# A PSUM tile of its own for each pair of output blocks, in a two-layer half-product stage on one NeuronCore

## The chip, the cores and the metric

The kernel runs on one core of one Trainium2 chip. The metric is device time in microseconds (us); the time given for a kernel is the median of its runs.

## What is computed

An attention with soft-capped scores feeds two feed-forward networks. Everything is float32 in and out.

```
q, k, v: (4 batches, 12 heads, 448, 64)
scores = cap * tanh(q k^T / 8 / cap);  attn = softmax(scores);  x = attn v -> (1792, 768)
h = x @ w_in (768 x 2048);  g = 0 | h | (h+1)^2/4 by range;  y = g @ w_out (2048 x 768)
m = max(y @ w1, y @ w2, y @ w3) (each 768 x 768);  out = m @ w_out2 (768 x 768)
```

## The kernel before

All activations are kept transposed: features in the 128 partitions, the 448 tokens of a batch in the free dimension. A matrix product in full precision is made of three TensorE products of rounded parts: high by high, high by low, low by high (three matmuls of a 128 x 128 weight block by a 128 x 448 operand). The high part is a copy to the type fp32r, the low part the difference.

The four batches come in three stretches. Batch 0 and then batch 1 run through `ffn`, block by block. Batches 2 and 3 (`last_two`) go through the four layers together, in `strassen`: each layer's product of 2 x 2 blocks is made of seven half products instead of eight, in seven stages. The rows of the two batches are the two halves of the tokens; output block m and output block m + n/2 make one **pair**. In `strassen` the pairs of a layer are taken in groups of three (`threes`): layer 0 has eight pairs (groups of 3, 3 and 2), layer 1 three, layer 2 nine, layer 3 three, which makes eight groups. In each of a group's seven stages every pair gets its own sum over K2 blocks of the operand (3 in layers 0, 2 and 3, 8 in layer 1), so a pair's share of a stage is 9 matmuls, or 24 in layer 1 (there in two runs of 12, with the other pairs between them).

Each pair has two accumulators in PSUM, chosen by `BANK = (0, 1, 0, 0, 1, 0, 1)`: stages 0, 2, 3 and 5 add into accumulator 0, stages 1, 4 and 6 into accumulator 1, "the second partial result". The pool `m` has three slots of one bank; accumulator 0 is an `m` tile for each pair (`ps_m` in the profile). Accumulator 1 comes from the pool `s`, which has two slots of two banks each (`ps_s`): one tile of two banks for two pairs, pair 0 in its first bank and pair 1 in its second, and another for pair 2. The attention stretches use the same pools: `s` for the scores, `a` (one slot of one bank, `ps_a`) for the products with v, `m` for row sums. After each stage each pair's sum is read out of PSUM ("landed", function `lander` and its like in `land_m`): stages 1, 4 and 6 by a VectorE addition or subtraction of two tensors (`plus`, recorded at the helper's line 261), stages 0, 2, 3 and 5 by a copy (line 256 on ScalarE, 258 on VectorE) or a VectorE maximum.

The weights of a stage are streamed (`stream`): a DMA on SyncE's queue brings a piece into a `wf` tile, a copy makes its high part in a `w` tile (line 256 or 258) and a VectorE subtraction its low part (line 261, `w<-wf,w`). There are four `w` slots; a piece feeds 18 or 9 matmuls, in layer 1 it feeds 12. The operands' own parts (`op`) are made once per layer by the same two operations (`divide`).

The order on every engine is planned ahead of time by `Plan`: operations have a cost, a due time (`want`) and dependencies, buffers are taken from pools in the order of their due times, and the planned order is written out as it is. In `strassen` a matmul operation depends on its operand, its weights, the earlier matmuls of its accumulator and the last landing of that accumulator of the same pair (`reads[i][x]`). The waits between engines are put in below the plan, by the framework, from which tiles an instruction reads and writes.

Of the kernel before, what the change touches and what calls it, by code (L numbers as in the profile page):

```python
# [20 lines left out]
class Plan:  # L21
# [29 lines left out]
    def op(self, cost, fn, want, deps=(), uses=(), takes=(), kind=None):  # L51
        o = Plan.Op()
        o.kind = kind
        o.cost, o.fn, o.want = cost, fn, want
        o.deps, o.takes = [d for d in deps if d is not None], list(takes)
        o.uses = list(dict.fromkeys([*uses, *takes]))
        for b in o.uses:
            b.users += 1
        for b in o.takes:
            self.order[b.pool].append((want, len(self.ops), b))  # L60
        o.n, o.out, o.t0, o.t1, o.e = 0, [], None, None, None
        self.ops.append(o)
        return o
# [131 lines left out]
def kernel(  # L195
# [17 lines left out]
    B, H, _, _, S = qk.shape  # L213
    D = 64
    P = 128
# [23 lines left out]
    def buf(p, name, shape, dtype=F32):  # L239
        return plan.buf(p, lambda: pools[p].tile(shape, dtype, tag=p, name=name))  # L240
# [725 lines left out]
    def strassen(layer, pos, swap, blocks, groups, land):  # L966
# [8 lines left out]
        def at(p):  # L975
            return begins(SOLO) + p * PART
# [67 lines left out]
        def stream(stage, pieces, w):  # L1044
            kind = STAGES[stage]
            n = RUN[layer]
            wf, wt = buf("wf", "wf", [P, WU]), buf("w", "w", [P, 2, WU], F32R)
            total = n * len(pieces)
            deps = []
            for m, r in pieces:  # L1050
                if kind[0] == "S":
                    deps.append(summed[layer, m, r][1][int(kind[1]) - 1])
                else:
                    deps.append(stored[corner(layer, m, int(kind[1]) - 1, int(kind[2]) - 1, r)[0]])

            def load(e):
                for x, (m, r) in enumerate(pieces):
                    if kind[0] == "S":
                        src = summed[layer, m, r][0][int(kind[1]) - 1]
                    else:  # L1060
                        u, o = corner(layer, m, int(kind[1]) - 1, int(kind[2]) - 1, r)
                        src = scratch[u][:, o : o + n]
                    nc.sync.dma_start(out=wf.tile[:, x * n : (x + 1) * n], in_=src)

            got = op({"Q": 1.7 * total / 1000}, load, w - 20, deps, takes=[wf])
            hi = op(
                c_copy(total / 1000),
                lambda e: copy(e, wt.tile[:, 0, :total], wf.tile[:, :total]),
                w - 9, [got], [wf], [wt],
            )  # L1070
            lo = op(
                c_tt(total / 1000),
                lambda e: tt(
                    e, wt.tile[:, 1, :total], wf.tile[:, :total], f32(wt.tile[:, 0, :total]),
                    ALU.subtract,
                ),
                w - 8, [got, hi], [wf, wt],
            )
            return wt, [hi, lo]

        for g, group in enumerate(groups):
            A = [buf("m", "ps_m", [P, 512]) for _ in group]
            wide = [buf("s", "ps_s", [P, 2, 512]) for _ in range((len(group) + 1) // 2)]

            def bank(x, i, A=A, wide=wide):
                if x == 0:
                    return A[i], (lambda: A[i].tile[:, :S])
                return wide[i // 2], (lambda: wide[i // 2].tile[:, i % 2, :S])

            taken = {}  # L1090
            last = [[None, None] for _ in group]
            reads = [[[], []] for _ in group]
            state = [land(m, g, i) for i, m in enumerate(group)]
            for stage in range(7):
                x = BANK[stage]
                begun = x == 0 and stage > 0 or stage == 6
                jobs = [(i, r) for r in range(runs) for i in range(len(group))]
                step = max(1, WU // RUN[layer])
                pos_ = starts[g][stage]
                ends = [None] * len(group)  # L1100
                for c in range(0, len(jobs), step):
                    piece = jobs[c : c + step]
                    wt, wops = stream(stage, [(group[i], r) for i, r in piece], at(pos_))
                    for y, (i, r) in enumerate(piece):
                        b_, get = bank(x, i)
                        for q in range(per):
                            k = r * per + q
                            a, aops = operands[stage][k]

                            def fn(e, y=y, q=q, a=a, k=k, get=get, wt=wt, begun=begun):  # L1110
                                o = y * RUN[layer] + q * P
                                wh, wl = (wt.tile[:, z, o : o + P] for z in range(2))
                                h, l_ = a.tile[:, 0], a.tile[:, 1]
                                start, stop = not begun and k == 0, k == K2 - 1
                                for z, (w_, x_) in enumerate(((wh, h), (wh, l_), (wl, h))):
                                    nc.tensor.matmul(  # L1116
                                        get(), w_, x_, start=start and z == 0,
                                        stop=stop and z == 2, skip_group_check=begun,
                                    )

                            deps = [*aops, *wops, *reads[i][x]]
                            if last[i][x] is not None:
                                deps.append(last[i][x])
                            take = [] if id(b_) in taken else [b_]
                            if not take:
                                deps.append(taken[id(b_)])
                            o = op(
                                {"T": PART}, fn, at(pos_), deps, [wt, a, b_], take, "layer",
                            )
                            last[i][x] = o  # L1130
                            taken.setdefault(id(b_), o)
                            pos_ += 1
                        ends[i] = o
                for i in range(len(group)):
                    b_, get = bank(x, i)
                    w = at(starts[g][stage] + (i + 1) * K2) + 0.1
                    r = state[i](stage, get, b_, ends[i], w)
                    reads[i][x] = [r] if r is not None else []
# [47 lines left out]
    def last_two():  # L1186
# [7 lines left out]
        def land_g(m, g, i):  # L1194
# [4 lines left out]
            return lander(G[m], G[m + NF // 2], int(swap), finish)  # L1199

        pos = strassen(0, 0, swap, blocks, threes(N2[0]), land_g)


# [4 lines left out]
        def land_y(m, g, i):  # L1208
# [3 lines left out]
            return lander(Y[m], Y[m + H2], int(swap), finish)  # L1212

        pos = strassen(1, pos, swap, list(zip(G, gdone)), threes(N2[1]), land_y)


# [4 lines left out]
        def land_m(x, g, i):  # L1221
# [45 lines left out]
            return go  # L1267

        pos = strassen(2, pos, swap, list(zip(Y, ydone)), threes(N2[2]), land_m)


# [73 lines left out]
```

## Time and profile before

| | before |
|---|---|
| median of 3 runs | 1025.92 us (1024.76 to 1026.2) |
| the profiled execution: time | 1023.67 us |
| the profiled execution: span from first to last instruction | 1021.5 us |
| TensorE (PE) busy | 984.8 us, 96% |
| VectorE (DVE) busy | 878.4 us, 86% |
| ScalarE (ACT) busy | 603.9 us, 59% |

The profile is of one execution. PE's busy time is made of matmul records that overlap: a matmul's record is longer than the distance to the next one, so a busy share near 100% is no proof that the matmuls stand as close as they can. Times within the trace are counted from the span's start.

### The profile page before, as it was taken

What the parts mean: (1) busy time and instruction counts of PE and PEld (TensorE: products, weight loads), DVE (VectorE), ACT (ScalarE), POOL (GpSimd) and SP (SyncE); (2) the same over time, 40 slices, a digit from 0 to 9 for tenths busy, and PEclk for the clock granted to TensorE, in tenths of its full rate; (3) what the DMA queues carried; (4) which work ended last, traced back from release to release, by engine and by line L of the source; (5) the groups of instructions that cost most, each with busy time, mean ns of one, the idle gap of its engine ahead of it and who ended that gap; (6) DMA issues with size and microseconds to landing.
All of it is one profiled execution on the core that took longest, in us unless ns stands there. A gap on an engine that the chain in (4) does not pass through costs nothing.

```text
span 1021.5 us, 14412 instructions
## 1 busy us (share of the span) xinstructions
PE 984.8 (96%) x5184; PEld 769.4 (75%) x5184; DVE 878.4 (86%) x1283; ACT 603.9 (59%) x916; POOL 81.8 (8%) x28
## 2 busy tenths in 40 slices
PE   7999999999999999999999999999999999999997
PEld 2224687787888777677777778888888898888886
DVE  5999999998998899998999989776999778657873
ACT  6877996676673788664655566655775325232331
POOL 2321011011010111111111110000000000000000
PEclk9999999999999999999999999999999999999999
DMA  6429979999886654465666555334233333333342
GB/s 166 126 85 320 280 226 293 289 295 336 271 306 234 185 155 150 140 198 192 225 206 196 170 168 184 94 95 130 76 93 103 114 111 101 93 116 93 94 136 89
DMA packets 89489, 177.05 MB, mean 173 GB/s; under 512 B 10698, under 2 KB 56394, under 8 KB 89418
## 3 DMA queue, kind: packets, MB, share of 16 engines
q1 hardware_dynamic: 89008, 176.05, 55.1%
q8 instruction: 40, 0.66, 0.3%
q14 instruction: 31, 0.25, 0.1%
q10 hardware_dynamic: 410, 0.08, 0.0%
HBM read 126.39 MB, written 49.63 MB: 172 GB/s over the span
## 4 chain that ended last, share of the span: by engine, by line
PE 60%; DVE 11%; issue 2%; ACT 2%; POOL 1%; DMA 0%; SPq 0%; DVEq 0%; POOLq 0%; ACTq 0%
PE ps_m L1116 18%; PE ps_s L1116 14%; PE ps_m L789 7%; PE ps_m L791 7%; PE ps_m L790 7%; PE ps_a L724 4%; PE ps_s L512 2%; DVE t L261 2%; DVE w L261 2%; POOL mb L556 1%; DVE G L261 1%; DVE ss L261 1%; DVE mx L261 1%; PE ps_r L603 1%; DVE op L261 1%
## 5 line engine op out<-in xcount | busy, mean ns | idle before, releaser
L256 ACT ACTIVATE w<-wf 128x768 fp32r<-128x768 f32 (+2 forms) x192 | 138.5, 723 | 161.5 <-PE ps_s L1116 60.6
L261 DVE TENSOR_TENSOR w<-wf,w 128x768 fp32r<-128x768 f32 (+2 forms) x255 | 207.3, 814 | 7.2 <-ACT w L256 5.0
L1116 PE MATMUL ps_m<-op,w 128*128 128x448 f32 x1008 | 208.9, 366 | 0.0
L1116 PEld LDWEIGHTS ps_m<-op,w 128*128 128x128 f32 x1008 | 189.3, 188 | 15.7
L1116 PE MATMUL ps_s<-op,w 128*128 128x448 f32 x756 | 163.9, 369 | 18.5 <-DVE G L261 7.0
L1116 PEld LDWEIGHTS ps_s<-op,w 128*128 128x128 f32 x756 | 140.1, 188 | 38.3 <-DVE G L261 10.4
L556 POOL PARTITION_ALL_REDUCE mb<-mx x24 | 81.6, 3400 | 532.3 <-DVE mx L261 488.0
L530 ACT ACTIVATE t<-ps_s,qscale 112x896 f32<-112x896 f32 x96 | 92.3, 1003 | 40.7 <-PE ps_s L512 31.4
L574 ACT ACTIVATE t<-t,cap_sb 112x896 f32<-112x896 f32 x96 | 95.7, 1038 | 15.3 <-DVE t L261 15.1
L261 DVE TENSOR_TENSOR t<-t,mb 112x896 f32<-112x896 f32 x96 | 99.4, 1083 | 3.4 <-POOL mb L556 3.4
L789 PE MATMUL ps_m<-y,w 128*128 128x448 f32 x216 | 81.1, 375 | 0.0
L790 PE MATMUL ps_m<-y,w 128*128 128x448 f32 x216 | 79.1, 366 | 0.8 <-DVE y L261 0.8
L791 PE MATMUL ps_m<-y,w 128*128 128x448 f32 x216 | 79.0, 366 | 0.0
L724 PE MATMUL ps_a<-t,v 112*64 112x448 f32 x384 | 78.9, 544 | 0.0
L789 PE MATMUL ps_m<-g,w 128*128 128x448 f32 x192 | 72.1, 375 | 0.0
L791 PE MATMUL ps_m<-g,w 128*128 128x448 f32 x192 | 70.3, 366 | 1.6 <-DVE w L261 1.6
L369 ACT ACTIVATE raw<-raw 128x768 f32<-128x768 f32 (+1 forms) x64 | 55.7, 872 | 26.5 <-DMA raw<-in_w 13.1
L790 PE MATMUL ps_m<-g,w 128*128 128x448 f32 x192 | 70.2, 366 | 0.0
L258 DVE CAST w<-wf 128x768 fp32r<-128x768 f32 (+2 forms) x63 | 29.3, 465 | 47.1 <-PE ps_m L1116 22.6
L261 DVE TENSOR_TENSOR mx<-mx,t 112x896 f32<-112x896 f32 x48 | 57.0, 1188 | 5.1 <-ACT t L530 2.8
L789 PE MATMUL ps_m<-x,w 128*128 128x448 f32 x156 | 59.0, 378 | 0.2 <-ACT h L256 0.2
L375 DVE SCALAR_TENSOR_TENSOR wf<-raw 128x768 int32<-128x768 int32 (+1 forms) x64 | 57.2, 893 | 1.9 <-ACT raw L369 1.1
(125 smaller groups left out, 1567.6 us busy)
## 6 DMA issues: line engine op xcount, KB each, us to landing
w<-wf SPq DMA_DIRECT2D x40, 384.0 KB
wf<-w SPq DMA_DIRECT2D x40, 384.0 KB
s<-ss SPq DMA_DIRECT2D x80, 192.0 KB
wf<-s SPq DMA_DIRECT2D x80, 192.0 KB
raw<-in_w SPq DMA_DIRECT2D x18, 768.0 KB
raw<-in_w_in SPq DMA_DIRECT2D x16, 768.0 KB
raw<-in_w_out SPq DMA_DIRECT2D x24, 512.0 KB
wf<-w SPq DMA_DIRECT2D x60, 192.0 KB
```

What stands on the lines that cost most here:

```text
L256: nc.scalar.activation(out=out_, in_=in_, func=AF.Copy)
L261: nc.vector.tensor_tensor(out=out_, in0=a, in1=b, op=o)
L369: nc.scalar.activation(out=hi, in_=hi, func=AF.Prelu, scale=2.0**-112, alpha=-(2.0**32))
L375: nc.vector.scalar_tensor_tensor(out=wf.tile[:, :n].bitcast(I32), in0=hi, scalar=3, in1=lo, op0=ALU.logical_shift_left, op1=ALU.bitwise_or,)
L530: nc.scalar.activation(out=t[c].tile, in_=ps.tile[:C, :, :S], func=AF.Tanh, scale=qscale[:C])
L556: nc.gpsimd.partition_all_reduce(out_ap=mb.tile.rearrange("p h s -> p (h s)"), in_ap=mx.tile.rearrange("p h s -> p (h s)"), channels=C, re ...
L574: lambda e, c=c: nc.scalar.activation(out=t[c].tile, in_=t[c].tile, func=AF.Exp, scale=cap_sb[:C]),
L724: nc.tensor.matmul(pa.tile[j * D : (j + 1) * D, :S], vt.tile[:, j, c], t[c].tile[:, j], start=start, stop=stop,)
L789: nc.tensor.matmul(ps.tile[:, :S], wh, a.tile[:, 0], start=start, stop=False)
L790: nc.tensor.matmul(ps.tile[:, :S], wh, a.tile[:, 1], start=False, stop=False)
L791: nc.tensor.matmul(ps.tile[:, :S], wl, a.tile[:, 0], start=False, stop=stop)
L1116: nc.tensor.matmul(get(), w_, x_, start=start and z == 0, stop=stop and z == 2, skip_group_check=begun,)
```

## The change

Accumulator 1 gets a tile for each pair. Pairs 0 and 1 of a group take a whole `s` tile each, of which they use the first bank; pair 2 takes the one-bank tile of the pool `a`. Pool sizes, operations, costs and due times stay as they are.

```diff
         for g, group in enumerate(groups):
             A = [buf("m", "ps_m", [P, 512]) for _ in group]
-            wide = [buf("s", "ps_s", [P, 2, 512]) for _ in range((len(group) + 1) // 2)]
+            wide = [
+                buf("s", "ps_s", [P, 2, 512]) if i < 2 else buf("a", "ps_a", [P, 512])
+                for i in range(len(group))
+            ]
 
             def bank(x, i, A=A, wide=wide):
                 if x == 0:
                     return A[i], (lambda: A[i].tile[:, :S])
-                return wide[i // 2], (lambda: wide[i // 2].tile[:, i % 2, :S])
+                if i < 2:
+                    return wide[i], (lambda: wide[i].tile[:, 0, :S])
+                return wide[i], (lambda: wide[i].tile[:, :S])
```

## Rows read from the trace of the kernel before

**Rows 1.** Stretches by engine: us, then busy us of PE, PEld, DVE, ACT, POOL, clock.
```profile
634.00:1017.90 383.90, 365.39 (x1766) 329.46 (x1765) 292.65 (x507) 169.70 (x310) 0.00 (x0) 1.00 0.34 104
634.00:646.30 12.30, 11.58 (x57) 10.41 (x57) 11.98 (x22) 10.24 (x20) 0.00 (x0) 1.00 0.41 129
717.50:772.00 54.50, 51.47 (x249) 46.18 (x248) 51.62 (x92) 38.52 (x73) 0.00 (x0) 1.00 0.31 88
776.70:805.90 29.20, 29.20 (x145) 27.07 (x145) 27.53 (x51) 18.99 (x36) 0.00 (x0) 1.00 0.39 109
```

**Rows 2.** PE's waits from 634 us on: us in total, times, longest us.
```profile
PE ps_s L1116 <- DVE G L261: 7.0, 9, 1.2
PE ps_s L1116 <- DVE M L261: 6.5, 9, 0.8
PE ps_s L1116 <- DVE Y L261: 2.7, 3, 1.3
PE ps_s L1116 <- DVE O L261: 2.2, 3, 0.8
```

**Rows 3.** Groups by form, 634 to 1018 us: busy us, mean ns | idle before.
```profile
L1116 PE MATMUL ps_m<-op,w 128*128 128x448 f32 x1008 | 208.9, 366 | 0.0
...
L1116 PE MATMUL ps_s<-op,w 128*128 128x448 f32 x756 | 163.9, 369 | 18.5 <-DVE G L261 7.0 <-DVE M L261 6.5 <-DVE Y L261 2.7
...
L261 DVE TENSOR_TENSOR M<-ps_m,M 128x448 f32<-128x448 f32 x6 | 3.7, 619 | 0.1
```

**Rows 4.** PE in order of time: start, us, count [idle before, releaser].
```profile
634.24 5.63 PE L1116 MATMUL ps_m<-op,w 128*128 128x448 f32 x27
...
672.86 3.31 PE L1116 MATMUL ps_s<-op,w 128*128 128x448 f32 x15 [1.16 <-DVE G L261]
676.00 5.63 PE L1116 MATMUL ps_m<-op,w 128*128 128x448 f32 x27
681.48 2.59 PE L1116 MATMUL ps_s<-op,w 128*128 128x448 f32 x12
684.79 3.31 PE L1116 MATMUL ps_s<-op,w 128*128 128x448 f32 x15 [0.72 <-DVE G L261]
687.93 11.11 PE L1116 MATMUL ps_m<-op,w 128*128 128x448 f32 x54
...
760.62 10.50 PE L1116 MATMUL ps_s<-op,w 128*128 128x448 f32 x51
772.37 4.52 PE L1116 MATMUL ps_s<-op,w 128*128 128x448 f32 x21 [1.25 <-DVE Y L261]
776.73 29.35 PE L1116 MATMUL ps_m<-op,w 128*128 128x448 f32 x144
...
1014.50 3.36 PE L1116 MATMUL ps_s<-op,w 128*128 128x448 f32 x15 [0.72 <-DVE O L261]
```

**Rows 5.** DVE in order of time, landings and one weight piece.
```profile
638.37 0.62 DVE L261 TENSOR_TENSOR X<-ps_a,rs 128x448 f32<-128x448 f32 x1
...
684.11 0.62 DVE L261 TENSOR_TENSOR G<-ps_s,G 128x448 f32<-128x448 f32 x1 [1.48 <-PE ps_s L1116]
...
686.35 0.62 DVE L261 TENSOR_TENSOR G<-ps_s,G 128x448 f32<-128x448 f32 x1
...
767.28 0.69 DVE L261 TENSOR_TENSOR w<-wf,w 128x512 fp32r<-128x512 f32 x1
...
771.69 0.63 DVE L261 TENSOR_TENSOR Y<-ps_s,Y 128x448 f32<-128x448 f32 x1
```

**Rows 6.** Matmuls of line 1116 into `ps_s`: ns min/median/max.
```profile
L1116 PE MATMUL ps_s<-op,w x756: 358/365/475, 639.7 to 1017.5; 128*128 128x448 f32 x189
```

**Rows 7.** Waits of the weight copies from 630 us on.
```profile
ACT w L256 <- PE ps_s L1116: 60.6, 27, 6.0
ACT w L256 <- PE ps_m L1116: 25.1, 25, 3.2
DVE w L258 <- PE ps_m L1116: 22.6, 22, 2.8
...
DVE w L258 <- PE ps_s L1116: 19.4, 16, 1.6
```

**Rows 8.** ACT in order of time, a high part made on a release.
```profile
765.73 0.63 ACT L256 ACTIVATE w<-wf 128x512 fp32r<-128x512 f32 x1 [1.80 <-PE ps_s L1116]
```

## The prediction

> **What bounds the kernel now.** I began with the stretches by engine, to find what the last two batches are limited by. From 634.0 to 1017.9 us, which is all of the half products, PE is busy 365.39 of 383.90 us and DVE 292.65, at the full granted clock of 1.00 (the 2.4 GHz level) [rows 1]. So PE sets the pace there, and 18.5 us of it are idle.
>
> Then PE's waits: the idle time is 24 waits, all before matmuls into `ps_s`, all ended by a DVE instruction that lands a result (9 + 9 + 3 + 3) [rows 2]. 24 is eight groups times the three stages of accumulator 1. The 1008 matmuls into `ps_m` waited for nothing [rows 3]. They are the control: the same operands, the same weight stream, landings after each stage too, six of them by DVE out of `ps_m` [rows 3], but a tile for each pair.
>
> Then the order of time, to see where in a stage the wait sits. Twelve matmuls into `ps_s` start at 681.48, then comes a wait, then 15 more from 684.79 [rows 4]. Twelve are the 9 of pair 0 and the first 3 of pair 1. DVE's landing of pair 0 had the engine idle for 1.48 us and yet started only at 684.11 [rows 5], 0.04 us after the twelfth matmul's end (681.48 + 2.59 = 684.07): it waited for pair 1's first three as well. Pair 1's fourth starts 0.06 us after the landing's end (684.73). Neither reads what the other writes; what they share is the tile. The 15 that follow hold six of pair 1 and nine of pair 2, and pair 1's landing at 686.35 [rows 5] falls among them without any wait: pair 2 has its own tile. In layer 1 the break is at 51 and 21 [rows 4]: 36 of the first run, 12 of pair 0's second run, 3 of pair 1, again one step into pair 1.
>
> **What one wait costs.** The idle column is less than the loss, since a matmul's record (365 ns at the median [rows 6]) is longer than the distance between two. That distance is (29.35 - 0.365) / 143 = 0.2027 us in the run of 144 [rows 4].
>
> - Idle as recorded: 7.0 + 6.5 + 2.7 + 2.2 = 18.4, or 18.5 unrounded [rows 2, 3].
> - The overlap that the break throws away: 0.365 - 0.203 = 0.162 us, 24 times: 3.9.
> - The restart: 15 matmuls should take 14 x 0.2027 + 0.365 = 3.20 and take 3.31 [rows 4]; one matmul in `ps_s` is as long as 475 ns [rows 6]. 0.10 us, 24 times: 2.4.
>
> Sum: 24.8 us. A second way: from 681.48 to 687.93 a stage takes 6.45 us where 27 x 0.2027 = 5.47 would do [rows 4], a loss of 0.98; 24 of these are 23.5, and the two long waits (1.16 and 1.25 against 0.72 [rows 4]) add 0.44 + 0.53, which makes 24.5. I take 24.7.
>
> The bounds: at least the idle time, 18.5, if nothing of overlap and restart came back. At most all that the stretch has over a gapless row of its 1764 matmuls: from the first one at 634.24 to 1014.50 + 3.36 = 1017.86 [rows 4] are 383.6 us; 1763 x 0.2027 + 0.365 = 357.7. That leaves 25.9.
>
> **The change, part by part.** *Removed*: the shared tile, and with it both halves of the false order (the landing waits for pair 1's three, pair 1 for the landing). The control in `ps_m` and pair 2 in `ps_s` show a tile of one's own without the wait. 24.7 us.
>
> *Added*: nothing is issued that was not before. Pair 0's landing, 0.62 us, now lies under pair 1's 9 matmuls, 1.82 us. If that cover were gone it would cost nothing either: that accumulator is next written one or two stages later, after 18 x 0.2027 = 3.65 us at the least (the group of two pairs).
>
> *Moved*: pair 2 goes from an `s` tile to the `a` tile. The first one waits for the last attention product to be read, which ends at 638.37 + 0.62 = 638.99 [rows 5]; its own first matmul comes after the 27 of stage 0, which starts at 634.24 [rows 4], and 18 of stage 1, not before 634.24 + 45 x 0.2027 = 643.36. 4.4 us of room, cost nothing. Later handovers have a whole stage and two pairs between them, 45 x 0.2027 = 9.1 us, less a landing that takes 0.62 and starts at most some 0.6 us late (the latest that I found: 771.69 against matmuls that ended at 760.62 + 10.50 = 771.12 [rows 4, 5]). The group of two pairs takes both `s` tiles instead of one; the next group wants them a stage later. Nothing. The plan never knew of the shared-tile wait (its dependencies go by pair), so I expect the order on each engine to stay.
>
> **What is late next.** The weights. Their high parts waited 90 times, 127.7 us in all, for PE to free a `w` tile [rows 7]: most pieces come as early as four tiles allow. In the densest stretch: a release by PE starts a copy at 765.73 [rows 8], its low part ends at 767.28 + 0.69 = 767.97 [rows 5], and PE needs it three pieces of 12 after the release, 7.3 us. The release is the end of the second piece of the stage that began at 760.62 [rows 4], 760.62 + 24 x 0.2027 + 0.16 = 765.6; 7.3 less 2.3 leaves 5.0 us of lead. This follows PE when PE is faster, as long as DVE has time. DVE is tight in 717.5 to 772.0: 51.62 of 54.50 us [rows 1]. Four waits go there (three of about 1.0 and one of 1.5, together 4.5), so PE wants 50.0 us and DVE needs 51.6: 1.6 us out of 5.0 of lead. At 634.0 to 646.3 DVE has 0.32 us spare against 0.98 lost: 0.7. Over the whole stretch DVE's 292.65 stands against 359. I cost it at nothing, with 2.3 us (1.6 + 0.7) at the other end.
>
> From 776.7 to 805.9 PE ran without any gap, at clock 1.00, with DVE busy 27.53 of 29.20 [rows 1]. That is the state the whole stretch should be in.
>
> A rule that speaks against the change: the Trainium skill (Perfetto Trace Analysis, Optimization Strategy) says that the same gap, repeated on an engine that should be saturated, can mean too little PSUM for the next tile. By that reading, taking whole two-bank tiles and using half would make it worse, and the sum would be zero or a loss. The row disagrees: the break is three matmuls into pair 1, in a tile long held, not ahead of a new tile's first matmul [rows 4].
>
> **The rivals.**
> - *DVE becomes the bound* where it is tight: the lead doesn't absorb the debt, 2.3 us come back, 24.7 - 2.3 = 22.4, 1003.5 us. For it 95% busy DVE in 717.5 to 772.0 [rows 1], against it the 5.0 us lead. 10%.
> - *Nothing changes*: the wait belongs to the pair order or the stage's subtraction, not to the tile, and stays. 1025.9 us. For it: all 24 are ended by a landing of accumulator 1, and those are always by DVE. Against it: pair 2's matmuls pass pair 1's landing, and six DVE landings out of `ps_m` stopped nobody [rows 3, 5]. 5%. The Trainium skill (PSUM — Partial Sum Buffer, PSUM bank collisions) asks for ordering by bank and quadrant; by it the two halves, in two banks, need no order, and the tile would not be the cause. The trace shows them ordered.
> - *Slower*: the one `a` tile. Each group's pair 2 must wait for the last group's landing of it, seven handovers counting the attention's. To be slower by 0.2% they must cost 24.7 + 2.1 = 26.8 us, 3.8 us each, so a landing would have to be 8.4 + 3.8 = 12.2 us late; the latest seen is 0.6. That would give 1028.0. 3%. The rule on repeated gaps that the Trainium skill has (Perfetto Trace Analysis, Optimization Strategy) would come to this here.
>
> **How the numbers follow.** My forecast, the waits gone and little or nothing in their place, has 82%. The sum is against the profiled execution: 1023.67 - 24.7 = 999.0 (span 996.8). The median of the runs is 2.25 us above that execution, so 1025.92 - 24.7 = 1001.2. Range: 1025.92 - 25.9 = 1000.0, and a microsecond for the runs' spread, 999.0; at the top 1025.92 - 18.5 = 1007.4, which holds the DVE rival too. A measurement of this kernel tells about 0.2%, 2 us. Faster: 82 + 10 = 92%; same 5%; slower 3%.
>
> **What would show it.** After the change: no wait of PE on a landing from 634 us on, runs of hundreds of matmuls, a stage of 27 in 5.47 us, the stretch in about 359 us, `ps_a` with 234 of the 756 matmuls, DVE's landings of pair 0 starting after nine matmuls. Wrong if `ps_s` keeps waits at a pair's third matmul, if PE waits on `w<-wf,w` around 750 to 775, or before the first matmul into `ps_a`.

## The result, and the profile after

The changed kernel takes 999.29 us (median of 4 runs, 997.94 to 1002.71) against 1025.58 us for the kernel before in the same comparison: ratio 0.9749, 95% interval 0.9721 to 0.9778. The forecast was 1001.2 us within 999.0 to 1007.4. The profiled execution took 1002.71 us; it is the longest of the four, and the last section has a reason for it that the prediction did not see coming.

The page of the changed kernel, its first lines, and the groups of matmuls (count | busy us, mean ns | idle us before them). Line 1116 is now line 1121:

```profile
span 1000.6 us, 14436 instructions
...
PE 982.5 (98%) x5184; PEld 770.8 (77%) x5184; DVE 876.6 (88%) x1283; ACT 602.2 (60%) x916; POOL 80.0 (8%) x28
...
L1121 PE MATMUL ps_m<-op,w 128*128 128x448 f32 x1008 | 211.2, 367 | 0.0
...
L1121 PE MATMUL ps_s<-op,w 128*128 128x448 f32 x522 | 111.7, 367 | 0.0
```

PE's idle time ahead of the `ps_s` matmuls is 0.0 us where it was 18.5 [rows 3], and the view of PE's waits has no entry from 634 us on where it had four [rows 2]. The other 234 of the 756 matmuls of accumulator 1 now go to `ps_a`. By stretches (columns as in [rows 1]), PE has no gap. DVE is busier than before in the stretch from 717.5 to 772.0 us; the work in it is not quite the same, since everything there now comes some 9 us sooner:

```profile
633.90:996.90 363.00, 363.00 (x1766) 330.98 (x1764) 289.52 (x506) 168.34 (x310) 0.00 (x0) 1.00 0.36 110
717.50:772.00 54.50, 54.50 (x266) 49.57 (x265) 53.80 (x97) 37.02 (x72) 0.00 (x0) 1.00 0.31 92
```

PE in order of time, columns as in [rows 4]. A stage of three pairs is one row of 18 and one of 9 with no wait in front, and the long runs go on from stage to stage:

```profile
633.95 5.63 PE L1121 MATMUL ps_m<-op,w 128*128 128x448 f32 x27
...
677.73 3.81 PE L1121 MATMUL ps_s<-op,w 128*128 128x448 f32 x18
681.37 1.98 PE L1121 MATMUL ps_a<-op,w 128*128 128x448 f32 x9
683.19 11.11 PE L1121 MATMUL ps_m<-op,w 128*128 128x448 f32 x54
...
725.18 3.88 PE L1121 MATMUL ps_s<-op,w 128*128 128x448 f32 x18
...
766.10 29.92 PE L1121 MATMUL ps_m<-op,w 128*128 128x448 f32 x144
...
994.88 2.02 PE L1121 MATMUL ps_a<-op,w 128*128 128x448 f32 x9
```

DVE's landings of that stage:

```profile
679.75 0.62 DVE L261 TENSOR_TENSOR G<-ps_s,G 128x448 f32<-128x448 f32 x1 [0.87 <-PE ps_s L1121]
...
681.99 0.62 DVE L261 TENSOR_TENSOR G<-ps_s,G 128x448 f32<-128x448 f32 x1
...
683.67 0.62 DVE L261 TENSOR_TENSOR G<-ps_a,G 128x448 f32<-128x448 f32 x1
```

Pair 0's landing starts at 679.75, just after its ninth matmul (677.73 + 8 x 0.2027 + 0.365 = 679.72), no longer after the twelfth. The order of the matmuls, and of DVE's and ACT's instructions, is the same in both traces, instruction by instruction, but for the name of the tile: the plan did stay. The same holds for every experiment below but the two that move one weight copy, so no difference between them comes from another order.

The stretch of the half products takes 994.88 + 2.02 - 633.95 = 362.95 us where it took 383.6 [rows 4]: 20.7 us won in this execution, not 24.7. What is missing is not a wait. A run of 144 matmuls takes 29.92 us here and took 29.35 before [rows 4]: the distance between two matmuls is (29.92 - 0.365) / 143 = 0.2067 us instead of 0.2027, with the granted clock at 1.00 in both. It starts to be longer at about 723 us and stays so to the end: 1322 matmuls, 0.0040 us each, 5.3 us.

### The profile page after: what moved, and what is told of

The parts are those of the page before. It is cut to its first block, busy times and chain, and to the rows that moved or that the text cites. A ratio compares the mean times of both kernels' runs of the same rounds, so it can differ in the third digit from the quotient of the medians.

```text
span 1000.6 us, 14436 instructions
## 1 busy us (share of the span) xinstructions
PE 982.5 (98%) x5184; PEld 770.8 (77%) x5184; DVE 876.6 (88%) x1283; ACT 602.2 (60%) x916; POOL 80.0 (8%) x28
## 4 chain that ended last, share of the span: by engine, by line
PE 76%; DVE 4%; ACT 1%; issue 1%; POOL 1%; DMA 1%; DVEq 0%; ACTq 0%; POOLq 0%
PE ps_m L1121 21%; PE ps_s L1121 11%; PE ps_m L789 10%; PE ps_m L791 10%; PE ps_m L790 9%; PE ps_a L1121 5%; PE ps_a L724 5%; PE ps_s L512 3%; PE ps_r L603 1%; DVE t L261 1%; POOL mb L556 1%; PE ps_s L523 1%; DVE mx L261 1%; DVE w L261 1%; DMA raw<-in_w_out 1%
## 5 line engine op out<-in xcount | busy, mean ns | idle before, releaser
L1121 PE MATMUL ps_m<-op,w 128*128 128x448 f32 x1008 | 211.2, 367 | 0.0
L1121 PE MATMUL ps_s<-op,w 128*128 128x448 f32 x522 | 111.7, 367 | 0.0
L1121 PEld LDWEIGHTS ps_s<-op,w 128*128 128x128 f32 x522 | 98.0, 188 | 9.4
L724 PEld LDWEIGHTS ps_a<-t,v 112*64 112x64 f32 x384 | 26.0, 137 | 42.7 <-issue 39.3
```

The lines of the kernel that those rows point to most:

```text
L724: nc.tensor.matmul(pa.tile[j * D : (j + 1) * D, :S], vt.tile[:, j, c], t[c].tile[:, j], start=start, stop=stop,)
L1121: nc.tensor.matmul(get(), w_, x_, start=start and z == 0, stop=stop and z == 2, skip_group_check=begun,)
```

## The experiments

All edits are to the changed kernel. Two things were to be told apart: what makes a shared tile cost a wait, and what sets the distance between matmuls.

**Pairs 0 and 2 share.** The tile still has two owners, but they are not neighbours in the order of matmuls.

```diff
-                buf("s", "ps_s", [P, 2, 512]) if i < 2 else buf("a", "ps_a", [P, 512])
-                for i in range(len(group))
+                buf("s", "ps_s", [P, 2, 512]),
+                *[buf("a", "ps_a", [P, 512]) for _ in group[1:2]],
...
-                if i < 2:
-                    return wide[i], (lambda: wide[i].tile[:, 0, :S])
+                if i % 2 == 0:
+                    return wide[0], (lambda: wide[0].tile[:, i // 2, :S])
-                return wide[i], (lambda: wide[i].tile[:, :S])
+                return wide[1], (lambda: wide[1].tile[:, :S])
```

> Pairs 0 and 2 share a two-bank tile, pair 1 has the one-bank tile; two pairs still share one tile in each group of three. Theory (the cost lies in a landing that falls while the other owner of the tile is issuing matmuls): pair 0's landing now falls under pair 1, which has its own tile, so no wait of PE on a landing from 634 us on, and the time is that of the changed kernel, 998 to 1003 us, ratio to before about 0.975. Rival (any tile with two owners costs a wait at each of its landings): 21 waits stay, seven groups of three times three stages, about 1020 us.

Measured: 1003.36 us (1000.76 to 1006.14), ratio 0.9793, interval 0.9768 to 0.9818. PE has one wait left of the 24, where the rival wanted 21 and the theory none. It is where DVE is tightest; PE's and DVE's rows of it:

```profile
763.84 2.59 PE L1121 MATMUL ps_a<-op,w 128*128 128x448 f32 x12
766.99 2.71 PE L1121 MATMUL ps_s<-op,w 128*128 128x448 f32 x12 [0.56 <-DVE Y L261]
```

```profile
766.23 0.61 DVE L261 TENSOR_TENSOR Y<-ps_s,Y 128x448 f32<-128x448 f32 x1
```

Pair 0's matmuls had ended at about 764.0, and DVE came to its landing 2.2 us later; pair 2's waited for it. In one more stage pair 0's landing, 1.1 us late, held a weight load of pair 2 for 0.36 us, and the matmul at 673.74 us came 0.14 us late; the other 19 stages show nothing. So a tile with two owners costs nothing as long as the landing of one is over before the other's turn. (The stretch took 363.2 us in this profile, 5.5 more than a gapless one at 0.2027: 4.5 because the matmuls stood 0.2067 us apart from 767 us on, the rest by the two places above. It also began at 637.12 us, against 633.95 to 635.62 in the three profiles of the changed kernel; why is open.)

**Pairs 1 and 2 share.** The same edit with the two-bank tile for pairs 1 and 2 (`i > 0`, `i - 1`) and the one-bank tile for pair 0.

> Pairs 1 and 2 share a two-bank tile, pair 0 has the one-bank tile. Theory: the waits come back, but 21 instead of 24 (none in the group of two pairs), and they move from three matmuls into pair 1 to three matmuls into pair 2: in a stage of 27 the break comes after 21, in layer 1 after 63 of 72. 21 times 0.98 to 1.0 us more than the changed kernel, 1018 to 1022 us, ratio 0.993 to 0.997. Rival (the wait belongs to the landing of a group's first pair): no waits, or at the old place after 12, and 998 to 1003 us or 1025 us.

Measured: 1013.95 us (1012.11 to 1015.08), ratio 0.9894, interval 0.9874 to 0.9914. The waits did move to three matmuls into pair 2, but there are 13 and not 21. PE's waits from 634 us on, then PE and DVE in order of time, a stage with the wait and one without:

```profile
PE ps_s L1121 <- DVE G L261: 3.8, 5, 0.9
PE ps_s L1121 <- DVE Y L261: 3.0, 3, 1.6
PE ps_s L1121 <- DVE sc L261: 1.4, 2, 0.7
PE ps_s L1121 <- DVE s L261: 0.9, 1, 0.9
PE ps_s L1121 <- DVE O L261: 0.7, 1, 0.7
PE ps_s L1121 <- DVE sv L261: 0.7, 1, 0.7
```

```profile
642.29 2.59 PE L1121 MATMUL ps_s<-op,w 128*128 128x448 f32 x12
645.59 1.48 PE L1121 MATMUL ps_s<-op,w 128*128 128x448 f32 x6 [0.72 <-DVE G L261]
...
671.62 3.81 PE L1121 MATMUL ps_s<-op,w 128*128 128x448 f32 x18
```

```profile
675.46 0.62 DVE L261 TENSOR_TENSOR G<-ps_s,G 128x448 f32<-128x448 f32 x1
...
676.54 0.62 DVE L261 TENSOR_TENSOR G<-ps_s,G 128x448 f32<-128x448 f32 x1
```

In the first stage the 12 are pair 1's nine and pair 2's first three, as expected. In the second, all 18 ran through, and the landing of pair 1, nine matmuls old, came at 675.46, just after pair 2's last ended (671.62 + 3.81 = 675.43). It is so in all eight stages without a wait: pair 1's landing starts 0.04 to 0.11 us after pair 2's last matmul. In the changed kernel, where nothing holds them, these same eight landings start within 0.35 us of that end, and the other 13 at least 0.88 us before it. My reading: in the eight the plan has the landing behind all of pair 2, so the tile's order delays the landing alone and PE has nothing left to wait for. The number was missed because I counted stages and did not look where the plan puts each landing.

**A tile for each pair in layers 2 and 3 alone.**

```diff
-            wide = [
-                buf("s", "ps_s", [P, 2, 512]) if i < 2 else buf("a", "ps_a", [P, 512])
-                for i in range(len(group))
-            ]
+            own = layer >= 2
+            if own:
+                wide = [
+                    buf("s", "ps_s", [P, 2, 512]) if i < 2 else buf("a", "ps_a", [P, 512])
+                    for i in range(len(group))
+                ]
+            else:
+                wide = [buf("s", "ps_s", [P, 2, 512]) for _ in range((len(group) + 1) // 2)]
...
+                if not own:
+                    return wide[i // 2], (lambda: wide[i // 2].tile[:, i % 2, :S])
```

> A tile for each pair in layers 2 and 3 alone, the shared tile as before in layers 0 and 1. Theory: 12 of the 24 waits stay, all before 850 us; 12 times 0.98 us are won, 1013 to 1015 us, ratio about 0.988. On the distance between matmuls (202.7 or 206.7 ns): if an interruption sets it and it then stays, then the uninterrupted stretch of layers 2 and 3, some 145 us, has one distance from its last interruption on, and slow stretches in layers 0 and 1 end at a wait; a slow one over all of layers 2 and 3 adds 2.8 us. Rival on the distance: it drifts by itself (heat, supply), then it changes at places where no wait or late weight load stands.

Measured: 1012.64 us (1010.88 to 1015.76), ratio 0.9882, interval 0.9851 to 0.9913: half the waits, half the gain, just under the 1013 us expected. PE in order of time:

```profile
715.92 3.36 PE L1127 MATMUL ps_s<-op,w 128*128 128x448 f32 x15 [0.72 <-DVE G L261]
...
722.84 2.64 PE L1127 MATMUL ps_s<-op,w 128*128 128x448 f32 x12
726.20 1.49 PE L1127 MATMUL ps_s<-op,w 128*128 128x448 f32 x6 [0.71 <-DVE G L261]
727.52 7.46 PE L1127 MATMUL ps_m<-op,w 128*128 128x448 f32 x36
...
774.07 4.60 PE L1127 MATMUL ps_s<-op,w 128*128 128x448 f32 x21 [1.24 <-DVE Y L261]
778.51 29.92 PE L1127 MATMUL ps_m<-op,w 128*128 128x448 f32 x144
808.27 10.70 PE L1127 MATMUL ps_s<-op,w 128*128 128x448 f32 x51
819.68 4.52 PE L1127 MATMUL ps_s<-op,w 128*128 128x448 f32 x21 [0.71 <-DVE Y L261]
...
849.84 4.52 PE L1127 MATMUL ps_s<-op,w 128*128 128x448 f32 x21 [0.72 <-DVE Y L261]
```

Twelve matmuls take 2.64 us before the wait at 726.20, as at 0.2067, and 36 take 7.46 after it, as at 0.2027. Again, 29.92 us for 144 and 10.70 for 51 between the restarts at 774.07 and 819.68, and 0.2027 from there on: through the last restart, at 849.84, and the 157 us without a break that follow. The distance changed at restarts and nowhere else.

**The changed kernel again, and one with a late weight load taken away.** In the changed kernel's trace one weight load came late just where the longer distance begins. PEld, two loads in one row: 0.46 us, where two take 0.40 right behind:

```profile
722.92 0.46 PEld L1121 LDWEIGHTS ps_m<-op,w 128*128 128x128 f32 x2
...
723.33 0.40 PEld L1121 LDWEIGHTS ps_m<-op,w 128*128 128x128 f32 x2
```

It is the first of pair 1 in stage 3 of layer 0's group of two, which needs the accumulator that ACT copies out from 722.61 to 723.14. In the next kernel one weight copy is planned behind that landing copy:

```diff
-        def stream(stage, pieces, w):
+        def stream(stage, pieces, w, after=()):
...
-                w - 9, [got], [wf], [wt],
+                w - 9, [got, *after], [wf], [wt],
...
+                    late = held if stage == 6 and len(group) == 2 else ()
-                    wt, wops = stream(stage, [(group[i], r) for i, r in piece], at(pos_))
+                    wt, wops = stream(stage, [(group[i], r) for i, r in piece], at(pos_), late)
...
+                if stage == 2:
+                    held = list(reads[-1][x])
```

> The changed kernel once more, profiled on its own, five rounds. Theory (a small interruption sets the distance between matmuls to 202.7 or 206.7 ns, and with the 24 breaks gone nothing sets it back): runs spread over 997.5 to 1003 us, and the profile's time follows from the us that it spent at the longer distance after 634 us, 2 percent of them on top of 997.5. Rival (noise of the host or of the DMAs): the spread has nothing to do with the distance, and a run at 202.7 ns throughout can be as long as one at 206.7.

> The changed kernel, with one copy of a weight piece in layer 0's group of two pairs planned behind the landing copy of stage 2 on ScalarE, so that pair 1's stage 3 finds its accumulator free about 0.8 us sooner and the weight load that came 0.06 us late at 723.2 us is in time. Theory (that late load set the longer distance for the remaining 273 us): no late weight load after 634 us, the distance stays what it was at 634 us, mostly 202.7, so 997 to 998.5 us in most runs and 1 to 3 us under the changed kernel's median. Rival (the distance changes by itself): the same spread as the changed kernel, 997.5 to 1003 us.

Measured: the changed kernel 1000.39 us (998.29 to 1004.03), ratio 0.9771, interval 0.9747 to 0.9796; the other 999.15 us (997.61 to 1000.97), ratio 0.9749, interval 0.9733 to 0.9766. First and last row of the stretch in the changed kernel:

```profile
635.62 5.63 PE L1121 MATMUL ps_m<-op,w 128*128 128x448 f32 x27
...
991.31 1.99 PE L1121 MATMUL ps_a<-op,w 128*128 128x448 f32 x9
```

991.31 + 1.99 - 635.62 = 357.68 us. The late load was there too, and this time the distance stayed at 0.2027. The theory then asks for 997.5 us; the execution took 999.11, and 1.7 of that lies before the half products (last section). Without the late load, the ACT rows show the landing copy ahead of the weight copy:

```profile
722.07 0.53 ACT L256 ACTIVATE G<-ps_m 128x448 f32<-128x448 f32 x1
722.49 0.84 ACT L256 ACTIVATE w<-wf 128x768 fp32r<-128x768 f32 x1
```

and two loads take 0.39 us there. Whether that kernel is faster is not settled: the intervals overlap, and one of its four runs, not most, lies in the 997 to 998.5 us that were expected.

**Both once more, and three waits put back.** A third kernel, run beside them, has the shared tile in layer 1 alone (`own = layer != 1` in the edit above).

> The kernel without the late weight load near 723 us, once more. Theory: the uninterrupted 1764 matmuls keep one distance from 634 us to the end; 357.7 us for the stretch if it is 202.7 ns. Runs mostly 997 to 1001 us; median 0.5 to 2 us under the changed kernel of the same call. Rival: same median and spread as the changed kernel.

> The changed kernel beside these two. Theory: runs in two kinds, about 998 and about 1001 to 1004 us, by whether the late weight load near 723 us sets the longer distance; in the profile the stretch takes 357.7 us or about 363, with nothing between unless the start is long too. Rival: a spread without relation to the distance.

> The changed kernel, but with the shared tile back in layer 1 alone: three waits of about 1.0 us (one of 1.5), near 770, 815 and 845 us. Theory of the distance (a restart sets it anew and it stays to the next one): a longer distance that begins at the late weight load near 723 us ends at the first of these waits, some 48 us later, and costs at most about 1 us there; the uninterrupted rest of 145 us can still be long after the last wait. So 3.5 us of waits, some 1001 to 1004 us, and in the profile every change of the distance after 634 us stands at one of the three waits or at the late weight load. Rival (the distance drifts by itself): changes elsewhere.

Measured: without the late load 998.88 us (998.02 to 999.58), ratio 0.9743, interval 0.9728 to 0.9758; the changed kernel 999.30 us (997.20 to 1000.70), ratio 0.9746, interval 0.9727 to 0.9765; three waits 1004.98 us (1003.32 to 1006.93), ratio 0.9805, interval 0.9787 to 0.9823. The first two again can't be told apart; both profiles have 357.7 us for the stretch. The third took 5.7 us more than the changed kernel, not 3.5. As expected, the longer distance began and ended at its waits (810.66 and 841.39). PE's rows of its first wait, then the stretches around it:

```profile
764.34 6.09 PE L1127 MATMUL ps_s<-op,w 128*128 128x448 f32 x21 [2.31 <-DVE Y L261]
...
810.66 4.60 PE L1127 MATMUL ps_s<-op,w 128*128 128x448 f32 x21 [0.72 <-DVE Y L261]
...
841.39 4.53 PE L1127 MATMUL ps_s<-op,w 128*128 128x448 f32 x21 [0.72 <-DVE Y L261]
```

```profile
764.30:765.40 1.10, 1.06 (x5) 1.01 (x6) 1.10 (x3) 0.00 (x0) 0.00 (x0) 1.00 0.02 6
765.40:769.00 3.60, 3.60 (x12) 3.18 (x11) 2.45 (x6) 1.67 (x3) 0.00 (x0) 0.53 0.25 73
769.00:799.00 30.00, 30.00 (x149) 27.84 (x149) 27.79 (x51) 19.53 (x37) 0.00 (x0) 1.00 0.37 106
```

That wait was 1.25 us before the change [rows 4] and is 2.31 us here, since DVE gets to the landing later when the nine waits of layer 0 are gone. After it PE's granted clock was 0.53 in the 3.6 us from 765.40 on, near the 1.2 GHz level, and the 21 matmuls took 6.09 us instead of 4.52. So this wait alone cost 1.59 us more than a usual one by its length and 1.57 by the clock, in this one profile; the runs without a profile don't show where their clock fell.

## Why the prediction was right

**What bounds the kernel.** Right: with the waits gone PE runs the stretch without a gap, at the distance that it had between the waits.

**The cause.** Right, and now shown by moving it, with the order on every engine unchanged: with pairs 1 and 2 sharing, the wait moves into pair 2; with pairs 0 and 2 sharing, all but one go, and that one has a landing that really was late. The cause is thus narrower than the change's words: not a tile shared by two pairs, but one shared by neighbours in PE's order whose landing falls between. The rule on repeated gaps from the Trainium skill (Perfetto Trace Analysis, Optimization Strategy) doesn't describe this case: no pool grew, and the gaps went, even with pairs 0 and 2 sharing, where a group holds three banks for accumulator 1 instead of the four of before.

**What one wait costs.** The sum of idle time, overlap and restart was 24.8 us, and I took 24.7. A stretch with neither waits nor the longer distance takes 357.7 us (four profiles), 25.9 less than before. Of these, 1.1 are the longer distance in the trace before (285 matmuls, 0.0040 us each, in five pieces). That leaves 24.8, or 1.03 us for each of the 24. With 12 and 13 waits left, the other two kernels give: 371.60 - 357.7 less 1.0 for the longer distance, 12.9 us for 12 waits; 373.79 - 357.7 less 2.0, 14.1 for 13. The 25.9 that stood in the prediction as the upper bound was this sum and the longer distance, which I had seen as a remainder and not looked into.

**Nothing in its place.** Right in the time, with less room in one place than I read from the trace. The 0.6 us by which the first landing in layer 1's second stage was late counts from the end of 51 matmuls, three of them pair 1's. Pair 0's own ended at 760.62 + 47 x 0.2027 + 0.365 = 770.51 [rows 4], so DVE was 1.2 us late there already before. In the changed kernel they end at about 758.66 + 11 x 0.2067 + 0.37 = 761.3 and DVE lands them here:

```profile
762.81 0.61 DVE L261 TENSOR_TENSOR Y<-ps_s,Y 128x448 f32<-128x448 f32 x1
```

1.5 us late; in the four profiles at 0.2027 throughout it is 2.2 to 2.4. So DVE fell back by 1.0 to 1.2 us where PE was as fast as forecast, and by 0.3 in the profiled execution, against the 1.6 that I put for 717.5 to 772. The lead took it up; the weights never stopped PE. But two experiments that hung a wait on this very landing paid for it, 0.56 and 2.31 us.

**Moved parts.** Right: no wait before a first matmul into `ps_a`, and the same order of instructions. The latest landing that I gave, 0.6 us, was not the latest (pair 1's come up to 1.5 us after their own matmuls in the trace before), and 9.1 less 0.62 is 8.5, not 8.4; the ones that free the `a` tile at a group's end start at most 1.0 us late in the changed kernel, so the room is as wide as forecast.

**The rivals.** DVE as the bound: the debt was there, no time came back. Nothing changes: excluded. The `a` tile: no wait on it.

**The time.** 999.29 lies 1.9 us under the forecast and inside the range, near its lower end. The range's lower end left one microsecond for the spread of runs; the changed kernel's 13 timed runs lie between 997.20 and 1004.03, and five of them under 999.0. That the median of four came out inside is in part luck: the longer distance, which the forecast did not know, lengthened at least one of the four.

## What to carry to other kernels

Where two accumulators live in one tile, look at whose matmuls are being issued when the other is read: under this framework the waits follow the tile, not the bank. One accumulator's readout then holds up the other's matmuls, and the other's matmuls hold up the readout. Take the loss from start to start of the instructions; the idle column alone held 18.5 of 24.8 us. After a wait is taken away, follow the instruction that used to end it: it may now come later, unseen as long as nothing hangs on it.

## What the runs showed that I had not expected

In the half products TensorE's matmuls of 448 columns stand either 0.2027 or 0.2067 us apart on average, at a granted clock of 1.00 in both cases. In the trace of the kernel before, columns as in [rows 4]:

```profile
919.14 3.36 PE L1116 MATMUL ps_s<-op,w 128*128 128x448 f32 x15 [0.72 <-DVE M L261]
922.34 5.74 PE L1116 MATMUL ps_m<-op,w 128*128 128x448 f32 x27
927.92 2.64 PE L1116 MATMUL ps_s<-op,w 128*128 128x448 f32 x12
931.28 3.31 PE L1116 MATMUL ps_s<-op,w 128*128 128x448 f32 x15 [0.72 <-DVE M L261]
```

27 matmuls take 5.74 us here and 5.63 elsewhere; the longer distance begins at the restart at 919.14 and ends at the next. Over the profiles of before, of the changed kernel and of the experiments, 12 of 53 restarts after a wait in the half products began a longer piece, and so did one of five passages of the late weight load (three of the changed kernel, one each with pairs 0 and 2 sharing and with three waits put back); none began or ended elsewhere. Without breaks a longer distance lasts: in the profiled execution of the changed kernel it cost 5.3 us over 273 us. That the choice falls at an interruption is shown by these places; what decides it, and whether it explains the whole spread of the runs that were timed without a profile, stays open. A kernel without the late load, run to test the latter, could not be told from the changed kernel.

The clock adds to the spread, too. Near 475 us PE has waits of 1.36 and 0.33 us in all ten profiles. In five of them, two of the changed kernel, the granted clock then fell to 0.50, the 1.2 GHz level, and the 16 matmuls behind them took 4.6 to 4.9 us instead of 3.23. That is before the half products and has nothing to do with the change; why it fell in five and not in the others stays open. It is not what makes the long runs: the three longest of the 13 (1002.71, 1003.25 and 1004.03 us) have a granted clock of 1.000 over the whole span.
